# Attention and a two-layer FFN on one core: a searched order of all operations, Strassen's second product in one more chunk, and a batch's pooled sums added by DMA in memory

## The chip, the cores and the metric

The kernel runs on one core of one Trainium2 chip, as one program. The metric is the device time of one execution in microseconds (us), lower being better. The core has TensorE (PE in the profile, with its weight loads in a row of their own, PEld), VectorE (DVE), ScalarE (ACT), GpSimd (POOL) and SyncE (SP, which here only issues DMAs), and 16 DMA engines that all queues share.

## What is computed

```python
q_d, k_d, v_d = (x.reshape(B, H, Sd, 4, D).mean(axis=3) for x in (q, k, v))   # B=8, H=8, S=576, D=64, Sd=144
out_up = np.repeat(softmax_attn(q_d, k_d, v_d), 4, axis=2)                      # pooled attention, spread again
mask = np.abs(pos[:, None] - pos[None, :]) < 4
out_local = softmax(where(mask, q @ k.T / 8, -1e9)) @ v                         # attention in a band
x = (out_up + out_local).transpose(0, 2, 1, 3).reshape(B * S, H * D)            # 4608 tokens x 512
h = x @ w_in                                                                    # 512 x 2048
g = where(h >= 1, h, where(h <= -1, 0, (h + 1) ** 2 / 4))
return g @ w_out                                                                # 2048 x 512
```

All is float32. The products of the FFN are made of three matmuls each, from operands split in a high and a low part of the type that TensorE takes at full speed (high by high, low by high, high by low).

## The kernel before

**Work and tiles.** The attention is done in 32 pairs of heads (8 batches `b` by 4 pairs `p`, pair `n = 4 b + p`). One pair is: loads of q, k and v; sums over four neighbouring columns of q and k (lines 430 and 435, on DVE) and over four rows of v (lines 629 and 632, on POOL); the scores on PE (lines 448 and 493); maxima, subtraction (line 557, on POOL), exponentials, sums and normalisation on DVE and ACT; transposes on PE (677, 702, 703); the products with v (755, 778); and the addition of both results into `xr`, a ring in SBUF of 1024 tokens (line 846, `o_x`). The FFN is done in 9 chunks of 512 tokens. Chunks 0 and 1 use plain products (lines 1132 and 1161). From chunk 2 on, the first product uses Strassen's scheme in Winograd's form (`winograd`, line 1344): seven products of halves in place of eight, for two of the sixteen 128-wide slices of the hidden layer at a time (`j` = 0 to 7). The second product is plain (`second`, line 1161: per `j` 24 matmuls of 512 columns), but in the chunks from `TWICE` on it too has seven products in place of eight (`twice`, line 1261: per `j` 42 matmuls of 256 columns). `TWICE` is `B - 1`, so chunks 7 and 8 do that. For it the sums of halves of `w_out` (`TA`, `TB`) are made beside the attention of pairs 14, 16, ... (`sums_of_second`) and kept in memory; all sums of `w_in` are kept there too, and chunk after chunk loads them again (`lA`, `lS`, `lTA`, `lTB`). `twice` gathers its seven sums in seven of the eight PSUM banks, and ends with `outputs` (lines 1284 and 1295). It therefore can't stand beside attention, which takes banks 0 to 2.

**Order.** Nothing is emitted directly. `plan.op` records each operation with its engine (or several), cost, dependencies, buffers and a due time (`key`, from `pos`, `pair_key` and the numbers in `K`). `Plan.run` is a list scheduler: it keeps a time for each engine, takes on the earliest engine the ready operation with the smallest due time among those that can start within `WINDOW`, and picks each buffer's place among the free ones. `emit` then writes the program in that order. On the chip each engine works through its own list in order, and waits on semaphores where an operand isn't there. SP's list holds all loads and stores but the chunks' outputs.

**The stretch of a batch.** `pair_key` puts batch 2 in chunk 1, batch 3 in chunk 2, and so on to batch 7 in chunk 6, 18.7 us apart by the plan within a chunk. `x_done[b, p]` is the operation that writes a pair's result; `sums_of_x` waits for it before it splits a chunk's tokens.

Of the kernel before, what the change touches and what calls it, by code (L numbers as in the profile page):

```python
# [8 lines left out]
F32 = mybir.dt.float32  # L9
# [36 lines left out]
NKB = SD // KB  # L46
KM = 112
# [8 lines left out]
TWICE = B - 1  # L56
JOBS = 14
# [4 lines left out]
class Buf:  # L62


    def __init__(self, pool, places, make):
        self.pool, self.places, self.make = pool, places, make
        self.users = 0
        self.units = None
        self.end = 0.0
        self.tile = None  # L70

# [20 lines left out]
class Plan:  # L92
# [7 lines left out]
    WINDOW = 0.15  # L100
    AHEAD = 0.25
    TO_PE = 0.04
    LATE = 0.10
    SWITCH = {(0, 1): 0.09, (1, 0): 0.22, (0, 2): 0.02, (2, 0): 0.17, (1, 2): 0.05, (2, 1): 0.05}
    FILL = 0.125
    FILL_MIN = 0.5
# [22 lines left out]
    def run(self):  # L129
        for o in self.ops:  # L130
            o.left = len(o.deps)
            o.next = []
        for o in self.ops:
            for d in o.deps:
                d.next.append(o)
        engines = ["PE", "ACT", "DVE", "POOL", "SP"]
        free = {"PE": 4.5, "ACT": 3.0, "DVE": 1.0, "POOL": 1.4, "SP": 0.75}
        ready = {e: [] for e in engines}
        avail, busy, users = {}, set(), {}
# [4 lines left out]
        def make_ready(o):  # L144
            for way in o.ways:
                t = 0.0
                for d in o.deps:
                    e = d.start if d in o.follows else d.end
                    if d.eng != way[0]:
                        e += self.PE_LATENCY if d.eng == "PE" else self.TO_PE if way[0] == "PE" else self.LATENCY  # L150
                        o.data = max(o.data, e)
                    t = max(t, e)
                if way is o.ways[0]:
                    o.since = t
                ready[way[0]].append((t, o, way))

        for o in self.ops:
            if not o.left:
                make_ready(o)

        def pick(b, taken):
            best = None
            for units in b.places:
                if any((b.pool, u) in busy or (b.pool, u) in taken for u in units):
                    continue
                t = max(avail.get((b.pool, u), 0.0) for u in units)
                if best is None or t < best[0]:
                    best = (t, units)
            return best

        self.done = []
        count = 0
        while count < len(self.ops):
            best = None
            for e in engines:
                cands = []
                for entry in ready[e]:
                    t, o, way = entry
                    t = max(t, free[e])
                    if way is not o.ways[0] and t + way[4] > max(free[o.ways[0][0]], o.since):  # L180
                        continue
                    if way[3]:
                        t = max(t, port_free)
                    if e == "SP":
                        t = max(t, dma_free - self.BACKLOG)
                    taken = set()
                    given = o.data
                    for b in o.bufs:
                        if b.units is None:
                            got = pick(b, taken)  # L190
                            if got is None:
                                break
                            taken.update((b.pool, u) for u in got[1])
                            end = got[0] + (self.TO_PE if e == "PE" else self.LATENCY)
                            given, t = max(given, end), max(t, end)
                    else:
                        o.late = self.LATE if e == "PE" and given > free[e] - self.AHEAD and (mode, o.mode) in ((0, 0), (0, 2)) else 0.0
                        cands.append((t, o, way))
                if cands:
                    t0 = min(c[0] + c[1].late for c in cands)  # L200
                    t, o, way = min((c for c in cands if c[0] + c[1].late <= t0 + self.WINDOW), key=lambda c: (c[1].key, c[1].n))
                    if best is None or t < best[0] or (t == best[0] and o is best[1] and way[1] < best[2][1]):
                        best = (t, o, way)
            if best is None:
                stuck = [(o.name, o.key) for e in engines for _, o, _ in ready[e]]
                raise RuntimeError(f"no work can go on: {stuck[:20]}")
            t, o, way = best
            for b in o.bufs:
                if b.units is None:
                    b.units = pick(b, ())[1]  # L210
                    for u in b.units:
                        busy.add((b.pool, u))
            o.eng, cost, o.fn, port = way[:4]
            o.start = t
            if o.eng == "PE" and free["PE"] < self.warm and t - free["PE"] > self.FILL_MIN:
                self.keep_warm(free["PE"], t, busy, avail)
            if o.eng == "SP":
                free["SP"] = t + self.ISSUE
                dma_free = max(dma_free, t + self.DMA_LATENCY) + cost
                o.end = dma_free  # L220
            else:
                if o.eng == "PE":
                    if o.after[0] is last:
                        cost = o.after[1]
                    last = o
                    cost += self.SWITCH.get((mode, o.mode), 0.0) + o.late
                    mode = o.mode
                free[o.eng] = t + cost
# [5 lines left out]
            for w in o.ways:  # L234
                ready[w[0]] = [x for x in ready[w[0]] if x[1] is not o]
            self.done.append(o)
            count += 1
# [7 lines left out]
            for n in o.next:  # L245
                n.left -= 1
                if not n.left:
                    make_ready(n)
        return max(o.end for o in self.done)

    def keep_warm(self, t0, t1, busy, avail):

        n = int((t1 - t0 - 0.25) / self.FILL)
        banks = [(avail.get(("ps", u), 0.0), u) for u in range(8) if ("ps", u) not in busy]
        if n < 1 or not banks or min(banks)[0] > t0 - 0.5:
            return
        u = min(banks)[1]
        o = Op(-1, [], [], [], 0.0, "fill")
        o.eng, o.fn, o.start, o.end = "PE", lambda: self.fill(u, n), t0, t0 + n * self.FILL
        avail["ps", u] = max(avail.get(("ps", u), 0.0), o.end)  # L260
        self.done.append(o)
# [10 lines left out]
def attention_then_ffn(ctx: ExitStack, tc, qT, kT, vw, vp, vq, band, fours, w_in, w_out, out):  # L272
# [80 lines left out]
    def pair_key(n):  # L353
# [7 lines left out]
        return pos[b - 1, 0] + K["p3"] + K["p3d"] * (n % NPAIR)  # L361

    x_done = {}
    summed = {}
# [6 lines left out]


    def attention(n):
# [24 lines left out]
        else:  # L398
            qk = sbuf("qk", [P, 2, S], F32, "qk", [0])
# [7 lines left out]
        if not by_pe:  # L407
# [11 lines left out]
        qdb = plan.buf("qd", [(0,), (1,)], lambda u: qd[u[0]])  # L419
        def sums_of(dst, src):  # L420
# [9 lines left out]
        o_qd = op("DVE", 0.75, lambda: nc.vector.tensor_reduce(  # L430
            qdb.tile[:, 0:SD], qb.tile.rearrange("p (s f) -> p s f", f=FACTOR), axis=AX.X, op=ALU.add),
            [l_q], [qdb, qb] + [hab] * (b < 2), kk[0], name=name + "qd",
            other=[("POOL", 1.17, lambda: sums_of(qdb.tile[:, 0:SD], qb.tile), True, K["qp" if first else "qp1"])] if b < 2 else [])
        kdb = scratch("kd", [P, SD], "kd")
        o_kd = op("DVE", 0.75, lambda: nc.vector.tensor_reduce(
            kdb.tile, kb_.tile.rearrange("p (s f) -> p s f", f=FACTOR), axis=AX.X, op=ALU.add),
            [l_k], [kdb, kb_] + [hab] * (b < 2), kk[0], name=name + "kd",
            other=[("POOL", 1.17, lambda: sums_of(kdb.tile, kb_.tile), True, K["qp" if first else "qp1"])] if b < 2 else [])
# [186 lines left out]

        vdb = scratch("vd", [P if shares else KB, NKB, P], "vd")

# [13 lines left out]
        if by_pe:  # L641
# [15 lines left out]
            def vd_out(copy):  # L657
# [4 lines left out]
                      other=[("DVE", 0.40, lambda: vd_out(nc.vector.tensor_copy), False, K["vv"])])  # L662
        elif shares:
# [176 lines left out]

        def add():
            s0 = 0
            while s0 < S:
                r = (b * S + s0) % RING
                m = min(S - s0, RING - r)
# [669 lines left out]
```

## Time and profile before

| | |
|---|---|
| Median of 3 runs | 916.5 us (916.1 to 919.12) |
| Time of the profiled execution | 915.25 us |
| Its span, from first to last instruction | 913.4 us |
| Mean granted clock of TensorE | 0.996 |

The profiled execution lies 1.25 us below the median. Outside its span it has 1.85 us. A page of the profile gives busy times by engine; the table by stage gives the same for stretches, here for the start (to 40.2 us, when the FFN's first matmul starts), for chunks 0 and 1 together (to 240.8), and then for each chunk, each taken from the first matmul of one chunk to that of the next.

### The profile page before, as it was taken

To read this page: it belongs to the slowest core of one execution; us is meant where nothing else is said; L and a number is where in the kernel's file an instruction comes from. 1 tells how busy PE (TensorE), PEld (TensorE's weight loads), DVE (VectorE), ACT (ScalarE), POOL (GpSimd) and SP (SyncE) were. 2 spreads that over 40 slices of the span, in tenths; PEclk is the share of its full clock that TensorE was granted. 3 is DMA by queue.
4 is the path that set the end of the run, shared out by engine and by line. 5 is a ranking of instruction groups with operands and counts; after the bars stand their busy time and mean duration, and the time that the engine had idled before them with its cause. 6 is when DMAs were issued, how large, how long until landed. Compare 5 with 4: busy or idle time off the path is not lost. (4 is left out here: it accounts for less than half of the span.)

```text
span 913.4 us, 21375 instructions
## 1 busy us (share of the span) xinstructions
PE 893.8 (98%) x8538; PEld 789.3 (86%) x8538; DVE 726.2 (80%) x1336; ACT 564.0 (62%) x1160; POOL 126.9 (14%) x124
## 2 busy tenths in 40 slices
PE   8699999999999999999999999999999999999998
PEld 7578888788898888888888888888898889999997
DVE  7899876899878679797877887787778687688767
ACT  4898986555465556555565556556556566575653
POOL 5123340111111100111111110221011000000000
PEclk9899999999999999999999999999999999999999
DMA  9996332664586758767686748776576448889882
GB/s 312 406 372 220 126 118 73 236 237 156 183 285 210 224 176 269 245 220 259 223 295 225 253 149 314 231 243 241 197 262 225 149 168 304 281 288 321 299 284 91
DMA packets 73227, 214.01 MB, mean 234 GB/s; under 512 B 8088, under 2 KB 11288, under 8 KB 73128
## 3 DMA queue, kind: packets, MB, share of 16 engines
q1 hardware_dynamic: 67864, 204.23, 65.3%
q10 hardware_dynamic: 5264, 8.42, 2.5%
q8 instruction: 67, 1.10, 0.5%
q14 instruction: 32, 0.26, 0.1%
HBM read 180.11 MB, written 32.51 MB: 233 GB/s over the span
## 5 line engine op out<-in xcount | busy, mean ns | idle before, releaser
L1161 PE MATMUL ps<-w_o,gt 128*128 128x512 f32 x1368 | 348.2, 395 | 0.5 <-DVE gt L1114 0.5
L1161 PEld LDWEIGHTS ps<-w_o,gt 128*128 128x128 f32 x1368 | 245.3, 188 | 47.2 <-DVE gt L1114 1.3
L1344 PE MATMUL ps<-T,lS 128*128 128x256 f32 x1008 | 149.0, 283 | 1.3 <-ACT tt L1350 1.3
L1344 PEld LDWEIGHTS ps<-T,lS 128*128 128x128 f32 x1008 | 132.4, 189 | 5.7 <-ACT tt L1350 2.9
L1350 ACT COPY tt<-ps 128x512 f32<-128x512 f32 x112 | 66.0, 589 | 68.5 <-PE ps L1344 66.0
L1344 PE MATMUL ps<-B,lA 128*128 128x256 f32 x672 | 101.6, 287 | 0.3 <-DVE tt L1353 0.3
L1344 PEld LDWEIGHTS ps<-B,lA 128*128 128x128 f32 x672 | 90.8, 189 | 9.5 <-DVE tt L1353 2.4
L1112 ACT CAST gt<-tt 128x512 fp32r<-128x512 f32 x108 | 67.1, 622 | 51.5 <-PE ps L1161 22.8
L1353 DVE TENSOR_TENSOR tt<-ps,tt 128x512 f32<-128x512 f32 x112 | 62.1, 554 | 44.0 <-PE ps L1344 42.9
L1132 PE MATMUL ps<-x,w_i 128*128 128x512 f32 x384 | 94.8, 396 | 2.0 <-DVE xr L846 1.5
L1098 ACT ACTIVATE tt<-tt 128x512 f32<-128x512 f32 x82 | 51.8, 631 | 60.3 <-DVE tt L1353 49.2
L1132 PEld LDWEIGHTS ps<-x,w_i 128*128 128x128 f32 x384 | 71.3, 188 | 19.3 <-DVE xr L846 1.8
L1114 DVE TENSOR_TENSOR gt<-tt,gt 128x512 fp32r<-128x512 f32 x108 | 77.2, 715 | 11.3 <-ACT gt L1112 9.1
L1110 DVE SCALAR_TENSOR_TENSOR tt<-tt 128x512 f32<-128x512 f32 x82 | 60.4, 737 | 21.9 <-ACT tt L1103 21.5
L1103 ACT ACTIVATE tt<-tt 128x512 f32<-128x512 f32 x114 | 72.1, 633 | 3.4
L632 POOL TENSOR_TENSOR vd<-vp 128x256 f32<-128x256 f32 (+1 forms) x30 | 22.8, 759 | 323.5 <-PE ps L778 297.8
L629 POOL TENSOR_TENSOR vp<-vp 128x512 f32<-128x512 f32 (+1 forms) x30 | 40.9, 1363 | 133.3 <-DMA vp<-vq 131.8
L1353 DVE TENSOR_TENSOR tt<-tt 128x512 f32<-128x512 f32 x56 | 39.8, 711 | 22.1 <-ACT tt L1350 22.0
L557 POOL TENSOR_TENSOR sl<-sl,mxl 128x640 f32<-128x640 f32 x29 | 39.7, 1370 | 98.3 <-DVE mxl L555 98.3
L1344 PE MATMUL ps<-B,lS 128*128 128x256 f32 x336 | 50.1, 285 | 1.6 <-DVE tt L1353 1.6
L1344 PEld LDWEIGHTS ps<-B,lS 128*128 128x128 f32 x336 | 45.8, 189 | 5.3 <-DVE tt L1353 2.0
L1344 PE MATMUL ps<-T,lA 128*128 128x256 f32 x336 | 48.8, 280 | 0.0
(145 smaller groups left out, 1450.3 us busy)
## 6 DMA issues: line engine op xcount, KB each, us to landing
lS<-S SPq DMA_DIRECT2D x112, 512.0 KB, 4.5
lA<-A SPq DMA_DIRECT2D x56, 512.0 KB, 4.7
vp<-vq SPq DMA_DIRECT2D x28, 512.0 KB, 5.2
lA<-A SPq DMA_DIRECT2D x56, 256.0 KB, 3.8
v<-vw SPq DMA_DIRECT2D x32, 320.0 KB, 4.6
raw_i<-w_in SPq DMA_DIRECT2D x16, 512.0 KB, 8.3
raw_o<-w_out SPq DMA_DIRECT2D x16, 512.0 KB, 8.9
qk<-qT SPq DMA_DIRECT2D x28, 288.0 KB, 4.1
```

What stands on the lines that cost most here:

```text
L557: o_s = op("POOL", 1.3, lambda: nc.gpsimd.tensor_tensor(slf(), slf(), ml_n(), op=ALU.subtract), [o_m], [slb, mlb], kk[2], name=name + "sub ...
L629: nc.gpsimd.tensor_tensor(vpb.tile[:, :, 0:2, :], vpb.tile[:, :, 0:2, :], vpb.tile[:, :, 2:4, :], op=ALU.add)
L1098: o2 = op("ACT", 0.49 + e, lambda: nc.scalar.activation(u(), src(), AF.Relu, bias=0.5, scale=0.5), deps, [srcbuf, ub], key, name=f"relu {n ...
L1103: nc.scalar.activation(u(), u(), AF.Square)
L1110: o4 = op("DVE", v, lambda: nc.vector.scalar_tensor_tensor(g(), src(), 1.0, u(), op0=ALU.max, op1=ALU.min), [o3], [srcbuf, ub], key, name= ...
L1112: o5 = op("ACT", 0.50 + e, lambda: nc.scalar.copy(flat(gb.tile[:, 0]), g()), [o4], [held, gb], key, name=f"gh {name}")
L1114: engine.tensor_tensor(flat(gb.tile[:, 1]), g(), flat(gb.tile[:, 0]), op=ALU.subtract)
L1132: nc.tensor.matmul(hb.tile[:, 0, :], wb.tile[:, w, cc * P : (cc + 1) * P], xt[:, x], start=cc == 0 and i == 0, stop=cc == NCC - 1 and i == 2)
L1161: nc.tensor.matmul(o, gb.tile[:, g, ts], wb.tile[:, w, :], start=i0 + i == 0, stop=i0 + i == 3 * nf - 1)
L1344: nc.tensor.matmul(xy(dst), l(w, k), yb.tile[:, v, k], start=first and n == 0, stop=n == 5, skip_group_check=True)
L1350: return op("ACT", cost, lambda: nc.scalar.copy(to(), src()), deps, [tb, XY], kx[i], name=f"{name} {c},{j}")
L1353: return op("DVE", cost, lambda: nc.vector.tensor_tensor(to(), a(), b(), op=ALU.add), deps, held, kx[i], name=f"{name} {c},{j}", port=port)
```

## The change

- `Plan.run` no longer chooses. It takes the order of all operations from a table (`ORDER`), the engine where there are two from another (`OTHER`), and each buffer's place from a third (`PLACES`), and only adds up the times.
- `TWICE` is `B - 2`: chunk 6 also does its second product by `twice`. So all attention has to be over by then. Batches 3 to 7 follow each other evenly through chunks 2 to 5, 18.0 us apart by the plan, and `twice` of chunk 6 waits for the last four results (`over`). Jobs of `sums_of_second` begin at pair 16.
- The ring of `xr` holds 1024 tokens only, so the tokens from `SPILL` = 3584 on (chunks 7 and 8) are written to a tile and from there to memory (`x_mem`), and loaded back into `xr` before their chunk.
- For batches 2 to 7 the sums over four of q, k and v are not made on DVE and POOL. The host lays out the four addends (`fourths`); a DMA of SP copies the first one to memory in memory (1.15 MB for a batch), and three DMAs of POOL, one after the other, add the others to it (`accum_op`). Each pair then loads its 287 KB (`sm`), in place of a load of 512 KB for v's sums. q, k and v themselves are still loaded.
- `qk` has two places in place of one; the scratch for POOL's DMA descriptors is set to 2048 bytes.

```diff
-TWICE = B - 1
-JOBS = 14
+TWICE = B - 2
+SPILL = NT - 2 * TOK
+JOBS = 16
...
+    def run(self, order, other, places):
...
+        for n in order:
+            o = self.ops[n]
+            e, cost, o.fn, port = o.ways[n in other][:4]
...
-        return pos[b - 1, 0] + K["p3"] + K["p3d"] * (n % NPAIR)
+        return pos[2, 0] + K["p3"] + K["p3d"] * (n - 3 * NPAIR)
...
+    def quarters_of(b, key):
+
+        op = plan.op
+        mem = dpool.tile([NPAIR, P, WIDTH], F32, name=f"sums_{b}")
+        rows = lambda a: a.rearrange("n k c -> (n k c)").rearrange("(r x) -> r x", r=P)
+        o = op("SP", 3.0, lambda: nc.sync.dma_start(rows(mem), rows(fourths[b - DIRECT, 0])), [x_done[b - 1, 0]], (), key, name=f"q0 {b}")
+        for f in range(1, FACTOR):
+            o = op("POOL", 0.9, lambda f=f: nc.gpsimd.dma_start(rows(mem), rows(fourths[b - DIRECT, f]), accum_op=ALU.add, max_dma_last_dim=2 * NPAIR * WIDTH),
+                   [o], (), key, name=f"q{f} {b}", landing=10.0, moves=6.0)
+        return o, mem
...
+        if quartered:
+            smb = sbuf("sm", [P, WIDTH], F32, "sm", [0, 1, 2])
+            qdb = Part(smb, lambda t: t[:, 0 : SD + D - QB])
+            vdb = Part(smb, lambda t: t[:, WIDTH - NKB * P :].rearrange("p (n c) -> p n c", n=NKB))
+            if b not in quarters:
+                quarters[b] = quarters_of(b, k0 - ld + K["ls"])
+            made, mem = quarters[b]
+            o_qd = o_kd = o_vd = op("SP", 0.75, lambda: nc.sync.dma_start(smb.tile, mem[p]), [made], [smb], k0 - ld, name=name + "ls")
...
+        if spill:
+            n_ = S * b + S - kept
+            spilled[b, p] = op("SP", 0.7, lambda: nc.sync.dma_start(x_mem[:, p, kept - SPILL : kept - SPILL + n_], spill.tile[:, 0:n_]), [o_x], [spill], kk[9], name=name + "sx")
...
+        over = [x_done[B - 1, i] for i in range(NPAIR)] if (c, j) == (TWICE, 0) else []
...
-            for n in range(c * NPAIR, min(c + 1, B) * NPAIR):
+            for n in range(c * NPAIR, B * NPAIR if c == TWICE else (c + 1) * NPAIR) if c <= TWICE else ():
...
-    total = plan.run()
+    total = plan.run(ORDER, OTHER, PLACES)
...
+ORDER = (
+    1, 4, 2, 6, 5, 7, 26, 29, 27, 30, 31, 32, 8, 9, 10, 78, 79, 84, 0, 53, 52, 83, 57, 82, 56, 11, 12, 36, 37, 3, 17,
...
```

What the tables and the new code do to the engines' lists is seen at three places.

**TensorE, the second slice pair of chunk 6.** Before (`lA1`, `lS12`, `lS34`, `lA22` are the loaded sums of `w_in`, `w_o` slices of `w_out`, `gt` the hidden layer's parts):

```order
L1344 MATMUL ps_90<-B11_5_6977,lA1_34_7461 128x256 x6
L1344 MATMUL ps_90<-T2_5_7466,lS12_34_7491 128x256 x6
L1161 MATMUL ps_90<-w_o14_1724,gt_89 128x512 x9
L1344 MATMUL ps_90<-B21_5_7483,lA1_34_7461 128x256 x6
L1344 MATMUL ps_90<-T3_5_7472,lS34_34_7499 128x256 x6
L677 MATMUL ps_90<-ident_66,sl_29_7639 128x128 x5
L702 MATMUL ps_90<-ident_66,sp_29_7683 112x128 x3
L703 MATMUL ps_90<-ident_66,sp_29_7683 128x128
L1161 MATMUL ps_90<-w_o1_690,gt_89 128x512 x6
L1344 MATMUL ps_90<-T1_5_7212,lS12_34_7491 128x256 x6
L1344 MATMUL ps_90<-T4_5_7580,lA22_34_7523 128x256 x6
L1161 MATMUL ps_90<-w_o1_690,gt_89 128x512 x3
```

And of the change (line 1337 was 1344, 1153 was 1161, 1254 was 1261; `g0`, `g1` are parts of sums of the hidden layer, `lTA` and `lTB` the loaded sums of `w_out`):

```order
L1153 MATMUL ps_90<-w_o12_1644,gt_89 128x512 x3
L1153 MATMUL ps_90<-w_o14_1709,gt_89 128x512 x6
L1337 MATMUL ps_90<-B21_5_6864,lA1_34_7795 128x256 x6
L1337 MATMUL ps_90<-T3_5_7839,lS34_34_7802 128x256 x6
L1254 MATMUL ps_90<-w_o1_675,gt_89 128x256 x6
L1254 MATMUL ps_90<-w_o0_661,gt_89 128x256 x6
L1337 MATMUL ps_90<-T1_5_6588,lS12_34_7800 128x256 x6
L1337 MATMUL ps_90<-T4_5_7798,lA22_34_7804 128x256 x6
L1254 MATMUL ps_90<-lTA_1_7971,g1_1_8002 128x256 x6
L1254 MATMUL ps_90<-lTB_1_7973,g0_1_8042 128x256 x6
L1337 MATMUL ps_90<-B22_5_7712,lS34_34_7802 128x256 x6
L1254 MATMUL ps_90<-lTB_1_7973,gt_89 128x256 x6
```

The transposes of pair 29 (counted from 1) are gone from this chunk, and its matmuls of 512 columns on `gt` have become groups of six of 256 columns, some with weights from `lTA` and `lTB`.

**GpSimd, in chunk 3 of before and chunks 2 and 3 of the change.** Before, for each pair the two sums of v and the subtraction of the maxima:

```order
L557 TENSOR_TENSOR sl_19_4569<-sl_19_4569,mxl_19_4584 128x640
L632 TENSOR_TENSOR vd_20_4771<-vp_18_4508 128x256
L629 TENSOR_TENSOR vp_19_4783<-vp_19_4783 128x2x256
L557 TENSOR_TENSOR sl_20_4878<-sl_20_4878,mxl_20_4893 128x640
L632 TENSOR_TENSOR vd_21_5055<-vp_19_4783 128x256
L629 TENSOR_TENSOR vp_20_5062<-vp_20_5062 128x2x256
L557 TENSOR_TENSOR sl_21_5249<-sl_21_5249,mxl_21_5260 128x640
L632 TENSOR_TENSOR vd_22_5443<-vp_20_5062 128x256
```

And of the change (line 529 was 557; line 329 issues an accumulating DMA into a batch's sums):

```order
L529 TENSOR_TENSOR sl_14_3010<-sl_14_3010,mxl_14_3012 128x640
L329 DMA sums_4_137<-fourths 256x1120
L529 TENSOR_TENSOR sl_15_3220<-sl_15_3220,mxl_15_3222 128x640
L329 DMA sums_4_137<-fourths 256x1120 x2
L529 TENSOR_TENSOR sl_16_3502<-sl_16_3502,mxl_16_3504 128x640
L529 TENSOR_TENSOR sl_17_3719<-sl_17_3719,mxl_17_3721 128x640
L329 DMA sums_5_142<-fourths 256x1120
L529 TENSOR_TENSOR sl_18_4024<-sl_18_4024,mxl_18_4026 128x640
L329 DMA sums_5_142<-fourths 256x1120
```

The sums of v are gone. Of the three accumulating DMAs of a batch, each has to wait for the one before it, and a subtraction that stands behind one stands behind its wait too.

**SyncE, in chunk 4.** Before (`vp` is v for the sums, `v` its windows, `qk` q and k of a pair):

```order
L412 DMA v_22_5445<-vw 128x640
L410 DMA vp_21_5450<-vq 128x1024
L1317 DMA lS34_20_5455<-S34_3_115 128x1024
L402 DMA qk_19_5515<-qT 128x576
L403 DMA qk_19_5515<-kT 128x576
L1317 DMA lA1_21_5527<-A1_4_116 128x1024
L1317 DMA lA22_21_5559<-A22_4_117 128x512
L1317 DMA lS12_21_5565<-S12_4_118 128x1024
L1317 DMA lS34_21_5585<-S34_4_119 128x1024
L1317 DMA lA1_22_5643<-A1_5_120 128x1024
L1317 DMA lA22_22_5673<-A22_5_121 128x512
```

And of the change, from the first load of batch 6's sums (line 387) on; the copy that begins these sums (line 327) stands 14 rows above it:

```order
L387 DMA sm_17_5620<-sums_6_147 128x560
L362 DMA qk_21_5387<-qT 128x576
L1310 DMA lA22_19_5636<-A22_2_111 128x512
L1310 DMA lA1_20_5748<-A1_3_114 128x1024
L1310 DMA lS12_20_5750<-S12_3_116 128x1024
L1310 DMA lS12_21_5815<-S12_5_124 128x1024
L1310 DMA lA22_20_5817<-A22_3_115 128x512
L1310 DMA lS34_20_5846<-S34_3_117 128x1024
L1071 DMA TA_3_143<-TAs_3_5584 128x1024
L363 DMA qk_22_5618<-kT 128x576
```

The load of 512 KB into `vp` is gone. The load of `sm` waits for the last accumulating DMA of its batch, and behind it on the same queue stand q, and the sums of weights for the slice pairs that follow.

## Rows read from the trace of the kernel before

**Rows 1.** The page: each engine's busy time, share of the span, instructions.

```profile
PE 893.8 (98%) x8538; PEld 789.3 (86%) x8538; DVE 726.2 (80%) x1336; ACT 564.0 (62%) x1160; POOL 126.9 (14%) x124
```

**Rows 2.** The table by stage: length, each engine's busy time, clock, DMA.

```profile
0.00:40.20 40.20, 30.01 (x528) 25.34 (x528) 30.37 (x53) 24.31 (x60) 14.40 (x29) 0.92 0.98 352
40.20:240.80 200.60, 199.56 (x1671) 160.43 (x1671) 172.43 (x307) 143.95 (x290) 45.76 (x38) 1.00 0.55 196
240.80:339.30 98.50, 98.24 (x994) 87.41 (x994) 73.37 (x134) 56.24 (x115) 13.19 (x12) 1.00 0.70 231
339.30:441.00 101.70, 99.69 (x997) 87.22 (x996) 86.33 (x153) 60.23 (x122) 14.26 (x12) 1.00 0.73 244
441.00:540.50 99.50, 98.94 (x997) 87.64 (x996) 80.34 (x149) 58.40 (x120) 14.55 (x12) 1.00 0.70 239
540.50:639.90 99.40, 99.00 (x998) 87.63 (x997) 78.96 (x144) 58.35 (x119) 14.61 (x12) 1.00 0.70 239
639.90:738.50 98.60, 98.60 (x997) 87.63 (x996) 75.08 (x139) 59.52 (x122) 10.14 (x9) 1.00 0.62 210
738.50:820.60 82.10, 82.10 (x655) 80.27 (x654) 59.50 (x123) 51.05 (x107) 0.00 (x0) 1.00 0.78 265
820.60:907.30 86.70, 85.87 (x704) 84.63 (x702) 67.17 (x137) 51.90 (x108) 0.00 (x0) 1.00 0.75 254
907.30:913.40 6.10, 1.77 (x8) 1.13 (x6) 2.67 (x5) 0.00 (x0) 0.00 (x0) 0.90 0.46 172
```

**Rows 3.** The waits of PE, longest first: total us, times, longest.

```profile
PE ps L688 <- DVE sp L622: 5.4, 1, 5.4
PE ps L1344 <- DVE tt L1353: 1.9, 2, 1.6
PE ps L1344 <- ACT tt L1350: 1.3, 3, 0.6
PE ps L1261 <- DVE tt L1284: 0.8, 1, 0.8
```

**Rows 4.** The timeline of PE in chunk 7: start, duration, instruction.

```profile
746.99 1.56 PE L1161 MATMUL ps<-w_o,gt 128*128 128x512 f32 x6
748.39 0.88 PE L1344 MATMUL ps<-B,lS 128*128 128x256 f32 x6
...
757.66 0.87 PE L1261 MATMUL ps<-lTA,g 128*128 128x256 f32 x6
758.37 0.88 PE L1261 MATMUL ps<-lTB,g 128*128 128x256 f32 x6
```

**Rows 5.** The stage table, lines 1161 (chunk 6) and 1261 (chunk 7).

```profile
639.90:738.50 98.60, 49.12 (x193) 34.07 (x192) 1.00 0.62 210
...
738.50:820.60 82.10, 37.66 (x282) 35.42 (x282) 1.00 0.78 265
```

**Rows 6.** The timeline of PE around one attention pair in chunk 2.

```profile
267.84 0.46 PE L448 MATMUL ps<-qk 64*64 64x64 f32 x16
...
281.87 0.80 PE L755 MATMUL ps<-al,v 64*64 64x61 f32 x40
...
287.33 0.46 PE L448 MATMUL ps<-qk 64*64 64x64 f32 x16
```

**Rows 7.** The groups by line and shape: the pooled sums, and POOL's subtraction.

```profile
L430 DVE TENSOR_REDUCE qd<-qk 128x144 f32<-128x576 f32 x28 | 20.9, 748 | 7.8 <-DMA qk<-qT 7.7
L435 DVE TENSOR_REDUCE kd<-qk 128x144 f32<-128x576 f32 x28 | 20.9, 746 | 0.3 <-DMA qk<-kT 0.3
L557 POOL TENSOR_TENSOR sl<-sl,mxl 128x640 f32<-128x640 f32 x29 | 39.7, 1370 | 98.3 <-DVE mxl L555 98.3
```

**Rows 8.** The DMA issues: queue, count, size, median us from issue to landing.

```profile
lS<-S SPq DMA_DIRECT2D x112, 512.0 KB, 4.5
raw_o<-w_out SPq DMA_DIRECT2D x16, 512.0 KB, 8.9
lA<-A SPq DMA_DIRECT2D x56, 256.0 KB, 3.8
```

More of the change, by code (lines that the diff above doesn't have):

```diff
@@ L46 @@
 NKB = SD // KB
+WIDTH = 2 * SD + D - QB + NKB * P
 KM = 112
@@ L103 @@
     LATE = 0.10
+    FREE = {"PE": 4.5, "ACT": 3.0, "DVE": 1.0, "POOL": 1.4, "SP": 0.75}
     SWITCH = {(0, 1): 0.09, (1, 0): 0.22, (0, 2): 0.02, (2, 0): 0.17, (1, 2): 0.05, (2, 1): 0.05}
-    FILL = 0.125
-    FILL_MIN = 0.5
     def __init__(self, warm=0.0, fill=None):
@@ L127, in op @@
         return o
[L129 to L139, printed above, removed]
+    def run(self, order, other, places):
+        free = dict(self.FREE)
+        avail, busy, users, done = {}, set(), {}, set()
         dma_free = port_free = 0.0
@@ L142, in run @@
         last = None
[L144 to L169, printed above, removed]
-        self.done = []
-        count = 0
@@ L173, in run @@
[L173 to L207, printed above, removed]
@@ new lines, in run, with pick @@
+        places = iter(places)
+        def pick(b):
+            units = b.places[next(places)]
+            assert not any((b.pool, u) in busy for u in units)
+            return max(avail.get((b.pool, u), 0.0) for u in units), units
+        self.done = []
+        for n in order:
+            o = self.ops[n]
+            e, cost, o.fn, port = o.ways[n in other][:4]
+            o.eng = e
+            assert n not in done and all(d.n in done for d in o.deps), o.name
+            done.add(n)
+            t = given = 0.0
+            for d in o.deps:
+                x = d.start if d in o.follows else d.end
+                if d.eng != e:
+                    x += self.PE_LATENCY if d.eng == "PE" else self.TO_PE if e == "PE" else self.LATENCY
+                    given = max(given, x)
+                t = max(t, x)
+            t = max(t, free[e], port_free if port else 0.0, dma_free - self.BACKLOG if e == "SP" else 0.0)
@@ L208, in run @@
             for b in o.bufs:
                 if b.units is None:
[L210 to L213, printed above, removed]
+                    x, b.units = pick(b)
+                    busy.update((b.pool, u) for u in b.units)
+                    x += self.TO_PE if e == "PE" else self.LATENCY
+                    given, t = max(given, x), max(t, x)
             o.start = t
-            if o.eng == "PE" and free["PE"] < self.warm and t - free["PE"] > self.FILL_MIN:
-                self.keep_warm(free["PE"], t, busy, avail)
@@ L244, in run @@
                         busy.discard((b.pool, u))
[L245 to L248, printed above, removed]
+        assert len(done) == len(self.ops)
         return max(o.end for o in self.done)
[L251 to L261, printed above, removed]
     def emit(self):
```

131 lines of the change are left out of this document (86 added, 45 removed), and 241 rows, old and new, of tables (ORDER, PLACES).

## The prediction

> **What bounds the kernel now.** I read the page first. PE is busy for 893.8 of 913.4 us, DVE for 80% and the others for less [rows 1]. The table by stage then shows where that does not hold [rows 2]. At the start PE is busy for 30 of 40.2 us, while the DMA engines are at 0.98; from 40.2 us on it is busy for all but about 5 us of 867; and after its last matmul some 6 us remain. So to the end of the FFN each microsecond of PE's work is one of the kernel's, and so is each wait that PE meets. The list of PE's waits is short [rows 3]: 5.4 us at one place in the start, and 1.9, 1.3 and 0.8 us behind it.
>
> A busy PE is not yet one at its pace, since its rows overlap. The pace is the distance between starts. In chunk 7 six matmuls of 512 columns start 746.99 and the next group 748.39, which is 1.40 us; six of 256 columns go from 757.66 to 758.37, 0.71 us [rows 4]. The clock is granted in full in every chunk (1.00), so these prices hold all along. With 336 matmuls of the first product and 192 of the second, a chunk of the middle needs 336 x 0.118 + 192 x 0.233 = 84.5 us without attention. Chunk 6 took 98.6 and chunk 7, with `twice` and no attention, 82.1 [rows 2].
>
> **The change part by part, in PE's time.**
>
> *The second product of chunk 6.* Per slice pair 24 matmuls of 512 columns become 42 of 256: 24 x 0.233 = 5.60 us become 42 x 0.118 = 4.97, so 0.63 less, and eight times that is **-5.0 us**. What chunk 7 showed bears it out: 98.6 - 82.1 = 16.5 us, of which 5.0 are this and 11.5 the four attention pairs, 2.9 us of PE each.
>
> *The attention of batch 7* goes from chunk 6 into chunks 2 to 5. Its 11.5 us of PE go with it: **0** in the sum. What must hold is that DVE carries five pairs where it carried four. In chunks 2 to 5 it is busy for 73.4, 86.3, 80.3 and 79.0 us [rows 2]. Even if a pair cost a quarter of all that DVE does in chunk 6 (75.1 / 4 = 18.8), which counts the FFN's part as the pair's, the worst of them would have 105, against about 104.6 of the stretch with a fifth pair in it. But 48 reductions for the sums of q and k leave DVE altogether, 0.747 us each [rows 7], 1.5 a pair and 7.5 in a chunk with five pairs. So it fits with that bound, and by more in truth. In chunk 6 DVE gets `twice`, as in chunk 7, where it was busy for 59.5 of 82.1.
>
> *The border between chunks.* `twice` keeps seven banks, and the next chunk's second products wait until `outputs` has read them. There was one such border (7 to 8) and PE waited 0.8 us there, for the last sum of `outputs` on line 1284 [rows 3]. Now there are two: **+0.8 us**. The wait of chunk 6's first sums for the last attention (`over`) lies behind 14 us of PE's own work in the list, against a chain of a few DVE and ACT operations under 1 us each; I cost it at nothing, and at most at 2.
>
> *The start.* The order there is new too. DVE begins at 3.9 us (the load of q) and is busy for 30.4 of the 40.2, so some 6 us of it are gaps, and PE's long wait of 5.4 us for DVE lies there [rows 2, 3]. The new list puts one more conversion of weights (about 0.7 us) ahead of the FFN's first matmul, and mixes the rest otherwise. If all gaps went it would give -5.3, if none +0.7. I take **-1.5**, nearer the second, since loads and chains of one pair stay as they are.
>
> *Waits in the middle.* Chunk 3 takes 101.7 us where chunks 2, 4, 5 and 6 take 99.0 in the mean, with DVE at its fullest, and 3.2 us of waits stand in the list for line 1344. An order that was chosen as a whole can take away most of that or put as much elsewhere: **-2**, between -5 and +3.
>
> *The sums by DMA.* POOL and DVE lose work that PE didn't wait for. What is new is a chain for each of batches 2 to 7: a copy and three accumulating DMAs of 1.15 MB, each after the landing of the one before, and then the `sm` loads, behind whose wait on SP stand the weights of the next slice pairs, while on POOL subtractions stand behind the accumulating DMAs. The trace has no accumulating DMA and no copy from memory to memory, so I bound it. From 256 to 512 KB the landing goes from 3.8 to 4.5 us, so 0.7 us for 256 KB [rows 8]; 1120 KB would land after 4.5 + 1.7 = 6.2 us, and an accumulation, which reads a second stream, after perhaps 9.3. Under full queues 512 KB took 8.9 us; in proportion 1120 KB take 19 and an accumulation 38. The chain takes 6 + 3 x 9.3 = 34 us at the low end and 133 at the high one. It has this room: 20 pairs now fill chunks 2 to 5, which took 399 us and get four pairs' PE time more, so 411 / 20 = 20.5 us a pair and 82 a batch. A pair goes from its scores to its result in about 17 us (14 from line 448 to line 755, then the addition) [rows 6], which starts the copy; less 4 for the `sm` load, 61 us remain. So the chain is hidden as long as an accumulation lands within (61 - 7) / 3 = 18 us. The share of the DMA engines in chunks 2 to 6 is 0.62 to 0.73, well off the 0.98 of the start, so I take a landing near the low end, 9 to 14 us, and **0**. A delay of the chain would first eat SP's lead: a slice pair lasts 98.5 / 8 = 12.3 us, and a load that is issued one slice pair ahead and lands in 4.5 has 8 us to spare.
>
> *The rest of the transfers.* The chains and `sm` add some 5.7 MB a batch and take 2.1 MB (the `vp` loads) away: 3.6 MB in 82 us is 44 GB/s, about as much again if an accumulation's second read counts, and a fifth pair's q, k and v in a chunk are 9 more. With 231 to 244 GB/s now in chunks 2 to 5 that is up to 340, where the start moved 352 and more. The spill of chunks 7 and 8 adds 4 MB. Weights may land later by some us; 0 in the sum, up to +4 in the range.
>
> The sum is -5.0 + 0.8 - 1.5 - 2 = **-7.7 us** on the profiled execution's 915.25, so 907.5. Its median lies 1.25 above; a part of that may show again, and I say **908 us**.
>
> **The rivals.**
>
> *The chain of sums is late (slower).* The place is the `sm` load on SP; the point from which it decides is a landing of 18 us. At 22 us each chain is 12 us over its room, 8 of them are covered, and PE loses 4 us in each of five batches: 20 us, so 928. For it speaks that full queues can make 38 of it; against it, that the queues were not full there.
>
> *The gain is eaten.* The lists are tighter: weights land later, and subtractions wait on POOL. A wait of 1.5 us in each of five batches is 7.5 us, and the time is 914 to 918. For it speaks that before PE has next to no waits for DMA to compare with, and POOL 98 us of waiting for DVE alone, in which a stall is seen by no one; against it the same 98 us, since they are room [rows 7].
>
> *More is gained.* The start loses all its gaps and the middle all its waits: -5.0 + 0.8 - 5.3 - 5 = -14.5, so 901. For it speaks that the whole order is new; against it that loads at the start stay at 0.98 of the DMA engines.
>
> *Weight loads set the pace.* The weight loads of the 192 matmuls in chunk 6 took 34.1 us, and 282 of those of `twice` 35.4, so 336 take 42.2 [rows 5]: 8.1 us more, where the starts say 5.0 less. Then the time would be 915.25 + 8.1 + 0.8 - 3.5 = 921. Against it: in chunk 7 weight loads fill 80.3 of 82.1 us and the chunk is still the shortest [rows 2]. The Trainium skill (Perfetto Trace Analysis, Identifying the Most-Contended Engine) tells one to judge TensorE by the busy share of its weight loads and not by that of its matmuls; by that rule this change is a loss. The distances between starts contradict it here.
>
> **How the numbers follow.** The forecast, 903 to 912, has 0.52; more gained (897 to 903) 0.14; the gain eaten 0.16, of which 0.04 is still faster, 0.09 within 0.3% (913.8 to 919.2, about what a measurement of this kernel can tell from no change) and 0.03 slower; the late chain 0.15, from 920 up; the weight loads 0.03. Faster is 0.52 + 0.14 + 0.04 = 0.70, the same 0.09, slower 0.03 + 0.15 + 0.03 = 0.21. For 8 in 10, what is left out is most of the late chain above 925 and a little below 898: the range is 898 to 925.
>
> **What would show it.** In the profile after, chunk 6 should last 82 to 84 us from its first matmul to that of chunk 7, and chunks 2 to 5 together about 408 to 412; the FFN's first matmul should start between 36 and 40 us. PE's matmuls should keep 0.233 and 0.118 us. The accumulating DMAs should land in 9 to 14 us, and no wait of PE should be for a load of weights or `sm` for more than a microsecond. I am wrong if SP stands at line 387 and PE's waits name `lA` or `lS`, if POOL's subtraction is late behind line 329 and ACT's exponential after it, or if the start goes beyond 41 us.

## The result, and the profile after

The changed kernel is slower: 925.25 us median of six runs (921.16 to 935.22), against 916.65 for the kernel before on the same chip, a ratio of 1.0076 with a 95% interval of 1.0053 to 1.0099. I had said 908 and faster. On another chip the ratio was 1.0158 (1.0121 to 1.0195), 931.42 against 917.47 us. The run of 935.22 us counts as a slow one and is left out of the first ratio; it was also the one profiled, so the profile read here is that of the second measurement (first kernel of the experiments), with a span of 927.9 us.

First the busy times of its page, which answer to [rows 1].

```profile
PE 897.9 (97%) x8682; PEld 800.4 (86%) x8682; DVE 713.8 (77%) x1354; ACT 566.8 (61%) x1197; POOL 96.2 (10%) x104
```

PE has next to the same work as before and is as full. Then the table by stage, as [rows 2], at this kernel's own borders: the start, chunks 0 and 1, and chunks 2 to 8 one by one; the columns are the same.

```profile
0.00:41.80 41.80, 31.66 (x528) 25.95 (x528) 30.27 (x53) 24.45 (x61) 14.21 (x30) 0.84 0.98 349
41.80:248.90 207.10, 204.40 (x1733) 164.75 (x1734) 163.14 (x298) 145.63 (x297) 45.82 (x43) 0.99 0.72 225
248.90:351.50 102.60, 100.31 (x1103) 88.77 (x1102) 75.36 (x137) 56.18 (x118) 9.81 (x9) 1.00 0.90 286
351.50:457.50 106.00, 102.82 (x1009) 90.27 (x1008) 81.99 (x152) 61.06 (x130) 8.50 (x7) 0.98 0.88 275
457.50:565.30 107.80, 103.26 (x1114) 90.61 (x1113) 79.73 (x151) 59.42 (x128) 10.89 (x10) 1.00 0.86 269
565.30:672.30 107.00, 104.04 (x1114) 92.20 (x1112) 84.50 (x157) 62.31 (x134) 6.97 (x6) 0.98 0.73 252
672.30:755.90 83.60, 83.60 (x714) 81.78 (x712) 63.35 (x130) 54.26 (x116) 0.00 (x0) 1.00 0.86 294
755.90:836.20 80.30, 80.30 (x674) 80.26 (x673) 66.19 (x140) 52.60 (x113) 0.00 (x0) 1.00 0.91 314
836.20:922.00 85.80, 85.80 (x704) 84.79 (x703) 66.81 (x139) 50.93 (x108) 0.00 (x0) 1.00 0.77 256
```

Chunk 6 is what the change promised: 83.6 us where it took 98.6. Chunks 2 to 5 together take 423.4 us and not some 411; chunks 3 to 5 have 3 to 4.5 us each in which PE is idle, and two of them show a clock of 0.98. Chunks 0 and 1 are 6.5 us longer, the start 1.6. Who makes PE stand there? Its own list of waits answers to [rows 3] (total, times, longest).

```profile
PE ps L1337 <- DVE tt L1346: 3.5, 2, 1.9
PE ps L621 <- DVE ps L577: 3.2, 1, 3.2
PE ps L1337 <- ACT tt L1343: 3.0, 3, 2.4
PE ps L1153 <- ACT tt L1167: 2.8, 1, 2.8
PE ps L730 <- ACT al L686: 2.3, 3, 1.0
PE ps L652 <- DVE sl L580: 2.0, 1, 2.0
PE ps L730 <- DMA v<-vw: 1.7, 1, 1.7
```

The waits at lines 621 and 652, and most of that for `al`, lie in the start. Of the loads only one of v is among them, near 106 us, and none of a weight; in chunks 2 to 5 it is almost only ACT and DVE that PE waits for, so one looks at what those wait for. ACT's list has two rows that stand out.

```profile
ACT tt L1167 <- DMA out<-tt: 14.6, 5, 4.1
ACT tt L1090 <- DMA out<-tt: 6.0, 3, 4.7
```

Line 1167 copies finished output from PSUM to a place in `tt`, line 1171 stores it to memory, and the next user of the place waits until the store has landed. One case in full, from the timeline of ACT in chunk 3:

```profile
366.41 0.59 ACT L1167 COPY tt<-ps 128x512 f32<-128x512 f32 x1
367.03 0.34 ACTq L1171 DMA_DIRECT2D out<-tt  x1
...
368.63 0.59 ACT L1167 COPY tt<-ps 128x512 f32<-128x512 f32 x1 [0.55 <-PE ps L1153]
369.25 0.34 ACTq L1171 DMA_DIRECT2D out<-tt  x1
...
373.62 0.59 ACT L1167 COPY tt<-ps 128x512 f32<-128x512 f32 x1 [2.99 <-DMA out<-tt]
...
380.52 0.59 ACT L1167 COPY tt<-ps 128x512 f32<-128x512 f32 x1 [4.08 <-DMA out<-tt]
```

and that of PE at the same place:

```profile
377.55 0.86 PE L1153 MATMUL ps<-w_o,gt 128*128 128x512 f32 x3
381.16 0.97 PE L1153 MATMUL ps<-w_o,gt 128*128 128x512 f32 x3 [2.75 <-ACT tt L1167]
382.30 1.40 PE L1153 MATMUL ps<-w_o,gt 128*128 128x512 f32 x3 [0.18 <-ACT gt L1104]
383.50 1.49 PE L1337 MATMUL ps<-B,lA 128*128 128x256 f32 x6
384.78 1.48 PE L1337 MATMUL ps<-T,lS 128*128 128x256 f32 x6
```

The third and fourth copies of the border want places of stores that have not landed: those issued at 367.03 and 374.24 land at 373.55 and 380.44, after 6.5 and 6.2 us. PE waits 2.75 us for the PSUM bank that the fourth empties. The last two rows show a second price: six matmuls of 256 columns take 1.28 us from start to start, not 0.71 as in [rows 4]. The table of short stretches shows the granted clock, 0.50, which is the level of 1.2 GHz, here and once more in chunk 5:

```profile
377.00:383.20 6.20, 3.27 (x15) 1.88 (x15) 0.86 (x2) 2.65 (x7) 0.00 (x0) 1.00 0.75 299
383.20:386.60 3.40, 3.40 (x15) 3.21 (x16) 2.43 (x6) 2.65 (x8) 0.00 (x0) 0.50 0.29 94
588.00:591.40 3.40, 3.40 (x14) 3.30 (x15) 0.69 (x1) 1.47 (x3) 0.00 (x0) 0.50 0.41 154
```

So the stall of 2.75 us here is followed by 3.4 us at half the clock, which cost 1.7 us more. Why do the stores land late? An accumulating DMA of line 329, issued at 360.95, was in flight beside the first of the two until 373.09. The second had none beside it, but the third copy was 3 us late by then, and so its store went out behind six loads of SP that it would have gone among. Of the 20 stores of line 1171 after 200 us, 17 have a landing in the trace: 9 had no accumulating DMA in flight on any part of their way and landed after 2.53 us (median), 8 had one and landed after 7.30. The same eight stores land after 2.57 us in the kernel without accumulating DMAs (second experiment); but the first two of them, near 265 us, are as late there (7.0 and 7.9), so not every late store is the sums' doing. The loads after 200 us are later beside an accumulating DMA too: `lS` 4.97 and 7.95 us, `lA` 4.81 and 7.57, `v` 5.85 and 9.38. The DMA issues of this kernel, to set beside [rows 8]:

```profile
lS<-S SPq DMA_DIRECT2D x112, 512.0 KB, 5.4
lA<-A SPq DMA_DIRECT2D x56, 512.0 KB, 5.5
sums<-fourths POOLq DMA_DIRECT2D x18, 1120.0 KB, 12.0
lA<-A SPq DMA_DIRECT2D x56, 256.0 KB, 4.6
```

### The profile page after: what moved, and what is told of

It is laid out like the page before. It is cut to its first block, busy times and chain, and to the rows that moved or that the text cites. A ratio compares the mean times of both kernels' runs of the same rounds, so it can differ in the third digit from the quotient of the medians.

```text
span 933.4 us, 21532 instructions
## 1 busy us (share of the span) xinstructions
PE 902.2 (97%) x8682; PEld 805.0 (86%) x8682; DVE 714.0 (76%) x1354; ACT 565.7 (61%) x1197; POOL 96.8 (10%) x104
## 3 DMA queue, kind: packets, MB, share of 16 engines
q1 hardware_dynamic: 72696, 217.99, 66.3%
q0 software_dynamic: 4896, 20.64, 12.1%
## 4 chain that ended last, share of the span: by engine, by line
PE 77%; DMA 9%; DVE 3%; ACT 3%; issue 1%; ACTq 0%; DVEq 0%; SPq 0%
PE ps L1337 27%; PE ps L1153 23%; PE ps L1254 12%; PE ps L1124 7%; DMA out<-tt 5%; PE ps L730 2%; DMA lS<-S 2%; PE ps L420 2%; DMA v<-vw 1%; PE ps L652 1%; DMA x_mem<-tt 1%; PE ps L753 1%; PE ps L465 1%; PE ps L677 1%; ACT tt L1167 1%
## 5 line engine op out<-in xcount | busy, mean ns | idle before, releaser
L1153 PE MATMUL ps<-w_o,gt 128*128 128x512 f32 x1176 | 308.1, 401 | 3.6 <-ACT tt L1167 3.4
L1153 PEld LDWEIGHTS ps<-w_o,gt 128*128 128x128 f32 x1176 | 213.1, 191 | 45.6 <-ACT tt L1167 3.9
L1337 PEld LDWEIGHTS ps<-T,lS 128*128 128x128 f32 x1008 | 135.2, 192 | 8.5 <-ACT tt L1343 3.4
L1124 PE MATMUL ps<-x,w_i 128*128 128x512 f32 x384 | 96.9, 402 | 2.1 <-DVE xr L826 1.2
L1106 DVE TENSOR_TENSOR gt<-tt,gt 128x512 fp32r<-128x512 f32 x95 | 68.0, 721 | 17.8 <-ACT gt L1104 17.3
L1104 ACT CAST gt<-tt 128x512 fp32r<-128x512 f32 x95 | 58.4, 619 | 33.5 <-DVE tt L1102 25.7
L1090 ACT ACTIVATE tt<-tt 128x512 f32<-128x512 f32 x66 | 41.7, 632 | 56.8 <-DVE tt L1346 51.7
L1095 ACT ACTIVATE tt<-tt 128x512 f32<-128x512 f32 x98 | 61.8, 631 | 2.2
L1206 ACT ACTIVATE tt<-tt 128x256 f32<-128x256 f32 (+1 forms) x69 | 33.7, 489 | 46.2 <-DVE tt L1346 44.5
L1102 DVE SCALAR_TENSOR_TENSOR tt<-tt 128x512 f32<-128x512 f32 x66 | 47.2, 718 | 10.9 <-ACT tt L1095 10.7
L562 ACT ACTIVATE sp<-ps,mxp 128x144 f32<-128x144 f32 x96 | 36.5, 381 | 19.7 <-DVE ps L572 11.1
```

The source lines that it names most:

```text
L1090: o2 = op("ACT", 0.49 + e, lambda: nc.scalar.activation(u(), src(), AF.Relu, bias=0.5, scale=0.5), deps, [srcbuf, ub], key, name=f"relu {n ...
L1095: nc.scalar.activation(u(), u(), AF.Square)
L1102: o4 = op("DVE", v, lambda: nc.vector.scalar_tensor_tensor(g(), src(), 1.0, u(), op0=ALU.max, op1=ALU.min), [o3], [srcbuf, ub], key, name= ...
L1104: o5 = op("ACT", 0.50 + e, lambda: nc.scalar.copy(flat(gb.tile[:, 0]), g()), [o4], [held, gb], key, name=f"gh {name}")
L1106: engine.tensor_tensor(flat(gb.tile[:, 1]), g(), flat(gb.tile[:, 0]), op=ALU.subtract)
L1124: nc.tensor.matmul(hb.tile[:, 0, :], wb.tile[:, w, cc * P : (cc + 1) * P], xt[:, x], start=cc == 0 and i == 0, stop=cc == NCC - 1 and i == 2)
```

## The experiments

The theories: **A**, the traffic of the sums makes other transfers land late, and their users have no slack for it. **B**, the searched order is too tight by itself, whatever the sums do. **C**, the chain of sums is waited for. The first four kernels ran on one chip with one set of runs of the kernel before (917.47 us).

**The changed kernel again** (no edit).

> The changed kernel itself once more, for a profile nearer its median of 925 us than the one at 933 and for its interval beside the others of this call. Every theory expects 921 to 928 us. Theory A (the DMA traffic of the sums lengthens landings) and theory B (the searched order leaves too little slack between an engine and the transfer behind it, whatever the sums do) and theory C (the chain of sums is waited for) all expect the loss in chunks 2 to 5, 15 us over 411 or more, with the copies of finished sums on ACT standing for the stores of out.

Measured: 931.42 us, ratio 1.0158 (1.0121 to 1.0195). Its profile is the one above.

**Without the accumulating DMAs.**

```
-        o = op("POOL", 0.9, lambda f=f: nc.gpsimd.dma_start(rows(mem), rows(fourths[b - DIRECT, f]), accum_op=ALU.add, ...
+        o = op("POOL", 0.9, lambda: None,
```

> The changed kernel without its 18 accumulating DMAs: the pooled sums of batches 2 to 7 hold one addend of four, everything else is done. Theory A (traffic) expects most of the loss in chunks 2 to 5 to go: 910 to 914 us, and store landings back to 4.2 us. Theory B (the order is tight by itself) expects no more than 2 to 3 us: 922 to 925. Theory C (waits for the chain) expects 910 to 916 as well, since a chain of one copy is never late.

Measured: 911.94 us, ratio 0.9940 (0.9916 to 0.9963), 19.5 us less. The table by stage, chunks 0 and 1 and then 2 to 5:

```profile
41.50:247.00 205.50, 203.19 (x1732) 163.62 (x1733) 163.72 (x298) 145.19 (x297) 42.00 (x37) 1.00 0.55 195
247.00:349.70 102.70, 100.25 (x1103) 88.73 (x1102) 75.50 (x137) 56.15 (x118) 6.30 (x5) 1.00 0.75 253
349.70:450.30 100.60, 100.35 (x1008) 88.97 (x1007) 81.70 (x152) 60.92 (x130) 5.90 (x4) 1.00 0.74 254
450.30:552.50 102.20, 102.08 (x1113) 90.66 (x1112) 80.07 (x152) 61.23 (x131) 6.59 (x5) 1.00 0.66 229
552.50:655.90 103.40, 102.54 (x1115) 90.80 (x1114) 84.13 (x157) 60.55 (x130) 6.88 (x5) 1.00 0.70 249
```

Chunks 2 to 5 take 408.9 us, 14.5 less, and ACT's wait at line 1167 is 4.8 us and not 14.6; the store of the third copy goes out at 369.56 and lands after 4.7 us. With the same order and the same places the loss is gone, so the order alone does not make it, and B falls. A and C remain.

**`sm` from the input.** All accumulating DMAs run; SP waits for none.

```
-            ... lambda: nc.sync.dma_start(smb.tile, mem[p]), [made], [smb], ...
+            ... lambda: nc.sync.dma_start(smb.tile, fourths[b - DIRECT, 0, p]), [made], [smb], ...
```

> The changed kernel with the copy and the accumulating DMAs as they are, but each pair's sm loaded from the input (one addend of four, so the sums used are not whole) and not from the summed memory: SP waits for no chain, the traffic is all there. Theory C expects 910 to 916 us, as without the accumulations. Theories A and B expect 922 to 926, no change.

Measured: 928.75 us, 1.0133 (1.0109 to 1.0157). SP had stood for the chain in the changed kernel, as this row of its waits says,

```profile
SPq L387 <- DMA sums<-fourths: 54.6, 5, 16.9
```

and the row is gone here, but the time stays (the intervals overlap). C falls for SP: its wait was long, and behind it nobody was late by enough. POOL stands for the chain too (96.7 us at line 329 in the changed kernel, 96.6 here), with subtractions behind it, but ACT's wait for a subtraction is the same with and without the accumulating DMAs, as this row of both profiles says:

```profile
ACT sl L531 <- POOL sl L529: 9.8, 5, 3.2
```

**The traffic alone, in the order of before.** A copy and three accumulating DMAs a batch, into spare memory, issued behind the addition (`x`) of a pair.

```
+            if o in self.more:
+                self.more[o]()
...
+        plan.more[x_done[b - 1, 0]] = lambda mem=mem, b=b: nc.sync.dma_start(rows(mem), rows(qT[b]))
+        for f in range(1, 4):
+            plan.more[x_done[b - 1, f]] = lambda mem=mem, b=b: nc.gpsimd.dma_start(rows(mem), rows(kT[b]), accum_op=ALU.add, ...
```

> The kernel before in its own order, with a copy and three accumulating DMAs of 1152 KB for each of batches 2 to 7 added, into spare memory that nobody reads, each issued behind the addition of a pair (so one a pair, and POOL seldom waits for the one before). Theory A expects it slower by 5 to 10 us: 922 to 927, with waits of ACT or PE behind DMA. Theory B expects 916 to 918, since the order of before has slack. Theory C expects 916 to 918 too, since nobody waits for these chains, so that C and A part here and in the kernel with sm from the input.

Measured: 1001.7 us, 1.0918 (1.0876 to 1.0959). A had the sign and missed the size by far. DVE's waits show why (first this kernel, then the kernel before):

```profile
DVE qd L432 <- DMA qk<-qT: 63.4, 18, 7.2
```

```profile
DVE qd L430 <- DMA qk<-qT: 7.7, 11, 2.0
```

The DMA goes out among the next pair's loads (one at 303.63 us, `vp` at 303.72, q at 308.35); after 200 us, q and k land after 9.6 and 10.4 us (median beside such a DMA) instead of some 5, and DVE stands with all that is queued behind the sum. So at these places the order of before has no more slack than the new one.

The next four kernels ran on a second chip (915.3 us for before). They ask by which transfer the changed kernel suffers, and what of an accumulating DMA hurts. The changed kernel itself did not run there; its ratio on the two other chips was 1.0076 and 1.0158.

**Without the stores of output in chunks 2 to 5.**

```
-                op("ACT", 0.40, lambda a=a, osb=osb: nc.scalar.dma_start(out[a : a + P, :], osb.tile), [o2], ...
+                op("ACT", 0.40, (lambda: None) if c in (2, 3, 4, 5) else lambda a=a, osb=osb: nc.scalar.dma_start(...), [o2], ...
```

> The changed kernel with all its accumulating DMAs, without the stores of finished output rows in chunks 2 to 5 (16 stores; those rows of the output are left out). Theory A, as it now stands: while an accumulating DMA is in flight a store of out lands after 7.3 us and not 2.4, the copy or activation on ACT that wants its tt place stands for it, and PE stands behind ACT. Then without these stores most of the 19.5 us that the kernel without accumulations gained comes back: 914 to 918 us. A rival (A2: it is the loads of v, q, k and weights, late by 3 to 4 us under an accumulating DMA, that PE meets) expects 926 to 930.

Measured: 913.87 us, 0.9980 (0.9964 to 0.9997). So the stores are the path, and A2 falls; but the traffic of 16 stores is gone here too, which the next kernel keeps.

**Own buffers for the copies.** The first two copies of a border go to the two halves of the place `vp0`, which stands empty in these chunks, the third to a new tile of 2 KB a partition.

```
+    def own(c, t, osb):
+        if c < DIRECT or t == 3:
+            return osb.tile
+        if t == 2:
+            return oc
...
+        return vs[c][:, t, :]
```

> The changed kernel, whole, with the same order and all its DMAs, but in chunks 2 to 5 three of the four copies of finished output go to buffers of their own instead of a place in tt, so that a late store holds back nobody. Theory A expects 915 to 920 us (the fourth copy still uses tt); rival A2 expects 926 to 931.

Measured: 915.08 us, 0.9997 (0.9976 to 1.0018). With every DMA and every store in place, chunks 2 to 5 take 408.6 us:

```profile
250.00:352.30 102.30, 100.25 (x1102) 88.71 (x1101) 75.35 (x137) 55.95 (x118) 9.80 (x9) 1.00 0.90 286
352.30:453.00 100.70, 100.45 (x1009) 89.04 (x1008) 81.64 (x152) 61.03 (x130) 8.46 (x7) 1.00 0.93 291
453.00:555.70 102.70, 102.12 (x1114) 90.60 (x1113) 79.62 (x151) 59.55 (x128) 10.80 (x10) 1.00 0.89 282
555.70:658.60 102.90, 102.52 (x1115) 90.83 (x1113) 84.48 (x157) 62.29 (x133) 7.03 (x6) 1.00 0.76 262
```

The stores and the loads of weights and of v still land late beside an accumulating DMA (7.54, `lS` 7.29, `v` 9.07 us), and in these chunks it costs next to nothing: PE's list has no wait for a load there. So what cost the time was the place in `tt` that a late store kept, not the lateness.

**Plain copies in place of the accumulating DMAs**, in the changed kernel and in the one before with its spare traffic.

```
-                     ... rows(fourths[b - DIRECT, f]), accum_op=ALU.add, max_dma_last_dim=2 * NPAIR * WIDTH)
+                     ... rows(fourths[b - DIRECT, f]), max_dma_last_dim=2 * NPAIR * WIDTH)
```

> The changed kernel with the 18 accumulating DMAs turned into plain copies of the same size on the same queue in the same places (the sums then hold the last addend alone). If what hurts is the second read and the addition of an accumulating DMA, 913 to 917 us and landings of some 8 us; if any transfer of 1120 KB at that place hurts, 924 to 930.

> The kernel before with a copy and three plain copies (not accumulating) of 1152 KB a batch into spare memory, at the places where the accumulating ones made it 84 us slower. If the addition is what hurts, 918 to 930 us; if any transfer of that size at those places does, 970 to 1000.

Measured: 912.22 us, 0.9961 (0.9932 to 0.9991), and 960.62 us, 1.0470 (1.0437 to 1.0504). The first says that it is the addition; the second fell between the two expectations: size and place alone cost the order of before 45 us, the addition some 40 more (84.2 less 45.3, on two chips). The pages' rows for POOL's queue, of the changed kernel and of the one with plain copies (packets, MB, share of the engines' time):

```profile
q0 software_dynamic: 4896, 20.64, 12.1%
```

```profile
q0 software_dynamic: 4896, 20.64, 6.3%
```

The same packets and megabytes hold the DMA engines twice as long when they add, and land after 12.0 us instead of 7.5.

The last two kernels ran on a third chip (915.75 us for before).

**The same spare traffic at another place** of the kernel before: accumulating again, but behind POOL's subtraction of a pair.

```
-            plan.more[x_done[b - 1, f]] = lambda ...
+            plan.more[sub_done[NPAIR * (b - 1) + f]] = lambda ...
```

> The kernel before with the same accumulating DMAs into spare memory that made it 84 us slower, but each issued behind POOL's subtraction of a pair, some 10 us later, when the next loads of vp, v, q and k are not yet due. If the place of such a DMA among the loads decides (theory A), most of the 84 us goes: 920 to 945 us. If the kernel before stands such a DMA nowhere, because it takes something from every transfer, 980 to 1005.

Measured: 933.12 us, 1.0186 (1.0165 to 1.0207). With the six copies where they were (their cost is in both figures), the same 18 accumulating DMAs make the kernel 84 us slower at one place and 17 at another; DVE waits 18.5 us for q where it waited 63.4:

```profile
DVE qd L433 <- DMA qk<-qT: 18.5, 13, 3.6
```

**Own buffers, and one DMA later.** With own buffers PE had one wait for a load, v near 105 us, which was under way with the second accumulating DMA of batch 2 (97.06 to 108.43 us):

```profile
PE ps L732 <- DMA v<-vw: 2.9, 1, 2.9
```

That DMA is moved behind the next operation of POOL, to 107.01 us.

```
+            if o.name == "q2 2":
+                held = o.fn
+                continue
             o.fn()
+            if held and o.eng == "POOL":
+                held()
+                held = None
```

> The changed kernel, whole, with three own buffers for the copies of finished output in chunks 2 to 5 as before, and the second accumulating DMA of batch 2 issued one row of POOL later (some 10 us), so that the load of v that PE met 2.9 us late near 104 us is no longer under it. Theory A expects the loss there to go too (3 us of wait and 1.7 us at the half clock): 909 to 913 us, 0.3% to 0.7% under the kernel before. If the wait near 104 us has another cause: 914 to 917.

Measured: 912.60 us, 0.9966 (0.9946 to 0.9986), as A expected. The wait near 105 us is not in its profile, and chunks 0 and 1 take 206.4 us where they took 209.9 with own buffers alone. The times by themselves don't show what the move is worth, since the two intervals overlap. Chunks 2 to 5 take 413.7 us in this profile (915.76 us, one of its longer runs), because in chunk 4 PE waits 1.9 us for ACT and then has 3.4 us at a granted clock of 0.50; why ACT is late there is not shown. This version computes all that the reference does and is faster than both kernels: by 0.3% than the one before, and by 1.1 to 1.9% than the changed one (their ratios to before compared).

## Why the prediction was wrong

**The step that failed** is "the rest of the transfers" with its "0 in the sum, up to +4", together with the "0" of the sums by DMA. In its place the runs show 19.5 us for the 18 accumulating DMAs, 14.5 of them in chunks 2 to 5. I asked whether the chain would be in time, and priced the sums as bytes (up to 340 GB/s where the start had moved 352). Neither was the question. An accumulating DMA landed after 12.0 us (median), within the 9 to 14 that I gave it, and the wait of SP behind it is as good as free (`sm` from the input). But for those 12 us it shares the 16 DMA engines with everything else, and as I had looked only at loads of weights, for which I had 8 us of lead, I overlooked the transfer with the least: the store of finished output, whose place in `tt` is wanted again 3 to 4 us after its copy began (366.41 to 370.63, 373.62 to 376.44). It landed after 2.53 us alone and 7.30 beside an accumulating DMA. Removing the DMAs gives 19.5 us; taking the place away from three of four copies gives back all that chunks 2 to 5 had lost.

In the Trainium skill (DMA: Bandwidth & Descriptors, Queues, rings and completion order) it says that each DMA engine serves the queues that have work in turn, packet by packet. What is seen here agrees with that: the store goes on ACT's queue and the sums on POOL's, and the store still takes 7.30 us where it took 2.53. A queue of its own did not protect it. That sentence would have told me to ask what else is in flight.

**The step that was right** is the work saved. Chunk 6 takes 83.6 us, in the 82 to 84 named, and 83.5 both without the accumulating DMAs and with own buffers; the pace is kept (0.71 us for six matmuls of 256 columns wherever the clock is full). Of the 15 us that chunk 6 got shorter, 11.5 are by my estimate the attention that moved and 3.5 remain, where the rival "weight loads set the pace" wanted 8.1 more; the pace that is kept refutes it, though weight loads fill 81.8 of the 83.6 us. (The section of the Trainium skill that I named there, Perfetto Trace Analysis, Identifying the Most-Contended Engine, sets the share of peak FLOPs beside the busy share of weight loads; I used the second alone.) Chunks 2 to 5 take 408.9 us without the accumulating DMAs and 408.6 with own buffers, in the 408 to 412 named; the moved attention and DVE cost what they should. The border that I put at +0.8 did not show: PE's list has no wait from chunk 6 on, and chunk 7 and what follows are 1.8 and 1.1 us shorter than before.

**The smaller terms.** The start got -1.5 us; the FFN's first matmul came at 41.8 us, beyond the 41 that I gave as a sign of being wrong, and in the profiles of its seven versions between 38.3 and 44.8, around the 40.2 of before. The stretch at a granted clock of 0.50 that begins near 30 us also differs, 6.8 us before and 13.7 here, so the term is nothing that a single profile can show. The waits of the middle got -2; the kernel without accumulating DMAs has 3.6 us of PE's waits in chunks 2 to 5, the kernel before 3.2, so the search removed none in sum. Chunks 0 and 1 got no term and take 205.5 us there instead of 200.6. PE is busy 3.6 us more in them, with 61 matmuls more: 52 are the scores of one more pair, and 9 are of the second product, which stood behind the border before (2.1 us at 0.233). And PE is idle 1.3 us more, with one wait of 1.5 us for v near 85 us. With these misses the time without the accumulating DMAs is 5.5 us under that of before on the same chip (911.94 against 917.47) and not 7.7.

**The rivals.** The late chain was to give 928 us, and the time came near it by another way: the chain was not late, its neighbours were. "The gain is eaten" came closest in kind, small waits behind later landings, but it named subtractions and weights and put the waits at half their size. The sign "PE's waits name `lA` or `lS`" would have missed the case, since in chunks 2 to 5 PE's list names ACT and DVE; what tells is the list of the engine that PE waits for. SP did stand at line 387, and it cost nothing that can be told from noise.

## What to carry to other kernels

A transfer that nobody waits for is not free: ask which transfers are in flight beside it and which of them has the least time between its landing and its next user; here it was a store whose buffer was wanted again. An accumulating DMA held the DMA engines here for twice the time of a plain copy of its size, and what it costs depends on its place and on the buffers beside it: 18 of them (and six copies) made the order of before slower by 84 us at one place and by 17 us at another. In the new order they cost 19.5 us, or, with three small buffers and one of them moved, nothing that the intervals tell from the kernel without them (0.9966 and 0.9940). Where PE's list of waits names another engine, read that engine's list before you form a theory.

## What was not expected of the hardware

The DMA engines were busy for 12.1% of the span with 20.64 MB of accumulating packets and for 6.3% with the same packets as plain copies; per megabyte SP's queue took 66.5% / 217.99 = 0.31% and the accumulating one 0.59%.

A stall of PE can cost more than its length. In the changed kernel the idle stretches of 2.75 us at 378.4 and of 2.44 us at 585.5 were followed by 3.4 us at the granted clock of 0.50, 1.7 us of work lost each; one of 1.93 us at 273.3 was not. In the kernel with own buffers and the later DMA one of 1.88 us at 525.8 was, so the length of the stall alone does not tell.
